# Attention and a gated two-layer product on one core: half sums moved to SBUF, two PSUM pairs, an immediate bias, a third feature buffer and another plan

## The chip, the core and the metric

The kernel runs on one core of one Trainium2 chip. A core has five engines that work side by side, each through its own instruction queue in order: PE (TensorE) multiplies matrices and writes only into PSUM, ACT (ScalarE) evaluates functions and copies, DVE (VectorE) does elementwise work, POOL (GpSimd) here issues DMAs and a few small writes, and SP (SyncE) issues DMAs. PSUM has eight banks of 128 partitions by 512 float32. The metric is the device time of one execution in microseconds, the lower the better.

## The reference, cut to what matters

There are 8 batches with 8 heads of 576 tokens and 64 features each. For each head

```python
q_p, k_p = phi(q, c, s), phi(k, c, s)        # relu(x) * cos(w), relu(x) * sin(w), side by side: 128 features
kv  = einsum('sf,sd->fd', k_p, v)            # 128 x 64
z   = sum(k_p, axis=s)                       # 128
num = q_p @ kv;  den = q_p @ z + 1e-6
attn = num / den
```

The result is laid out as x, 4608 tokens by 512 features, and goes through

```python
h = x @ w_in           # 512 -> 2048
g = h * cos(h)
out = g @ w_out        # 2048 -> 512, float32
```

Inputs and output are float32; on the chip the matmuls take float16 and sum in float32.

## The kernel before, in words

**Tiling.** A batch's 576 tokens are 4 tiles of 128 and a rest of 64. The rests of two batches share a tile, so all rests together form a ninth chunk of 512 tokens. The gated product therefore runs over nine chunks: chunk c is batch c for c below 8, and chunk 8 holds the rests.

**Attention of a batch.** `load` (L354) brings q, k and v by DMA on SP into one raw buffer each, which the next batch uses again. `prep` (L377) makes the features kp and qp, as Relu with a scale on ACT (L386) or as max and multiply on DVE (L387). `cast_v` (L391) casts v. `kv` (L405) sums 8 heads of k features times v and a column of ones (L413) and copies the result to kvz (L425, L427 or L430). The q features are transposed, for the first two batches by PE (`q_pe`, L436), later by DMA (`q_dma`, L450). `num` (L459) computes numerator and denominator in two banks of PSUM (L474) and a DVE norm after it: the denominator (L490), its reciprocal (L492) and the product (L494). The result x is transposed into xT, for batches 0 to 2 by PE (`x_pe`, L507), later by DMA (L522).

**The gated product of a chunk.** `layer1` multiplies by w_in: in column pieces of 256 tokens for chunks 0 and 1 (L561), as whole tiles (L593) for chunk 2, and for the chunks after that half as whole tiles and half by a scheme of seven products of half size instead of eight (`layer1_fast`, L663, matmuls on L695), with intermediate sums on ACT (L703) and DVE (L707). `gate` (L531) takes cos as a sine with a bias of pi/2 that lies in a column of SBUF, PIH, on ACT (L534), and multiplies on DVE (L536) into gT. gT exists twice; chunk c uses gT[c % 2], chunk 8 gT[0]. `layer2` multiplies by w_out, also with seven products (L849), with sums of gT parts on DVE (L831, L876) and results gathered in ost by ACT (L860) and DVE (L864). Only chunk 0 uses `layer2_plain` (L776): for each of four token tiles a first half of eight matmuls (j below 8) and a second half, which sum up in the same bank (L789); the four tiles hold M2_0, M2_1, TR and M1_2 until the second half is done, and then ACT copies each to ost (L796).

**PSUM.** M1_0 to M1_2 and TR serve layer 1 and transposes, M2_0 and M2_1 layer 2, and ATT, two banks wide, the attention. Batch 0's four numerators are spread over pairs of these banks, `PAIRS` (L319), and batch 1's all use ATT.

**Order.** No engine order is written out by hand. Each piece of work is a step of `Plan` (L17), with an engine, an estimated cost, a due time, and the buffers that it reads and writes. `forward` (L92) lays the steps out in time by keys, `backward` (L191) derives new keys from how late each step could be, and `run` (L71) repeats this 12 times and keeps the order with the earliest end. Steps with several engines, such as preps, take the engine that ends first. This happens while the program is built, not on the chip. The first step sequence is `first_attention`, `layer1(0)`, `late_q0`, `second_attention`, `layer2_plain(0)`, `layer1(1)`, `w_out_sums` (L801), and then attention, `layer2` and `layer1` per chunk. w_out arrives in quarters; its second half waits behind batch 1's loads (`rest_of_w_out`, L949).

Of the kernel before, what the change touches and what calls it, by code (L numbers as in the profile page):

```python
# [16 lines left out]
class Plan:  # L17
# [11 lines left out]
    PASSES = 12  # L29
# [11 lines left out]
    def add(self, eng, occ, lat, due, fn, rd=(), wr=(), dma=None, lane=None, late=0.0,  # L41
            lazy=None):
# [17 lines left out]
        for key in wr:  # L60
# [6 lines left out]
                               lazy=lazy))  # L67
# [3 lines left out]
    def run(self):  # L71


        key = [s["due"] for s in self.steps]
        best = None
        for _ in range(self.PASSES):
            start, done = self.forward(key)
            end = max(done)
            if best is None or end < best[0]:
                best = (end, start, done, [s["eng"] for s in self.steps])  # L80
            key = self.backward(start, done, end)
        for s, a, b, e in zip(self.steps, best[1], best[2], best[3]):
            s["start"], s["end"] = a, b
            s.update(zip(("eng", "occ", "lat", "fn"), s["opts"][e]))
        return sorted(self.steps, key=lambda s: (s["start"], s["n"]))
# [6 lines left out]
    def forward(self, key):  # L92
# [13 lines left out]
        ready = {e: [] for e in self.LINK}  # L106

# [20 lines left out]
        while todo:  # L128
            best = None
            for e, cand in ready.items():  # L130
                if not cand:
                    continue
                limit = max(free[e], min(avail[n] for n in cand)) + self.PATIENCE.get(e, 0.0)
                k, t, n = min(((key[n], max(free[e], avail[n]), n) for n in cand
                               if avail[n] <= limit and first(n, e, max(free[e], avail[n]))),
                              default=(0, 0, None))
                if n is None:
                    rest = [(max(free[e], avail[n]), n) for n in cand
                            if first(n, e, max(free[e], avail[n]))]
                    if not rest:  # L140
                        continue
                    t, n = min(rest)
                if best is None or t < best[0]:
                    best = (t, e, n)
# [28 lines left out]
            free[e] = t + s["occ"]  # L173
            if n in follow:
# [59 lines left out]
def kernel(  # L234
# [57 lines left out]
    kp = sb("kp", [P, NT + 1, H, 2, D])  # L292
    qp = sb("qp", [P, NT + 1, H, 2, D])
# [9 lines left out]
    gT = [sb(f"gT{n}", [P, NJT, SM]) for n in range(2)]  # L303
    NCH = 4
# [13 lines left out]
    LEAD = 32.0  # L318
    PAIRS = [(BANKS[0], BANKS[1]), (BANKS2[0], BANKS2[1]), None, (BANKS[2], BANKS[3])]  # L319

# [4 lines left out]
    ORDER0, ORDER1, HOLDW = "qkv", "kqv", 1  # L325
# [12 lines left out]
    def dve(occ, due, fn, rd, wr, lat=0.13, lazy=None):  # L338
        pl.add("DVE", occ, occ + lat, due, fn, rd, wr, lazy=lazy)
# [4 lines left out]
    def either(due, cost, fn, rd, wr):  # L344

        lat = {"DVE": 0.13, "ACT": 0.15, "POOL": 0.15}
        pl.add([(e, cost[e], cost[e] + lat[e], fn[e]) for e in cost], 0, 0, due, None, rd, wr)
# [183 lines left out]
    def gate(bank, key, dst, dkeys, due):  # L531
        c = chn[0] % NCH
        chn[0] += 1
        act(0.59, due, lambda: nc.scalar.activation(  # L534
            out=ch[c], in_=bank, func=AF.Sin, bias=PIH, scale=1.0), [key, "PIH"], [("ch", c)])
        dve(0.61, due, lambda: nc.vector.tensor_tensor(  # L536
            out=dst, in0=bank if len(dst.shape) == 2 else bank.rearrange("p (j s) -> p j s", j=dst.shape[1]),
            in1=ch[c] if len(dst.shape) == 2 else ch[c].rearrange("p (j s) -> p j s", j=dst.shape[1]),
            op=ALU.mult), [key, ("ch", c)], dkeys)
# [47 lines left out]
    def layer1_plain(c, j, X, xk):  # L587
# [8 lines left out]
        gate(M, mk, gT[c % 2][:, j, :], [("g", c % 2, j, t) for t in range(NT)], due + 1.5)  # L596
# [3 lines left out]
    SUMS_AT = min(FAST1) - 1  # L600
    CH2, JF = NCT // 2, JH * P // 2
# [11 lines left out]
    n2 = CH2 * JF  # L613

    def wsum(ap, n):
        return ap[:, n * n2:(n + 1) * n2].rearrange("p (c f) -> p c f", c=CH2)
    WSB = {n: wsum(flat(kp if n in (2, 3) else qp), n % 2) for n in range(1, 5)}
# [9 lines left out]
    def w_in_sums(f, due):  # L627
# [3 lines left out]
        gone = {nm: [(nm + "p", t, g, h) for t in range(NT + 1) for g in range(2) for h in range(H)]  # L631
                for nm in "kq"} if f else {"k": [], "q": []}
        ws = WSB if f else WSA

        def tt(n, a, b, op, rd, wr):
            dve(0.61, due, lambda: nc.vector.tensor_tensor(out=ws[n], in0=a, in1=b, op=op),
                [("w_in", f), ("w_in", 2 + f)] + rd, wr + [("WS", n, f)], lazy=20.0)
        tt(3, a11, a21, ALU.subtract, [], gone["k"])
        tt(1, a21, a22, ALU.add, [], gone["q"] if f else [("w_in", 2)])
        tt(2, ws[1], a11, ALU.subtract, [("WS", 1, f)], [])  # L640
        tt(4, a12, ws[2], ALU.subtract, [("WS", 2, f)], [])

# [3 lines left out]
    def layer1_sums(c, X, xk):  # L646
# [6 lines left out]
        def tt(n, a, b, rd, wr=()):  # L653
            dve(0.33, start[c] - 1 + 0.3 * n, lambda: nc.vector.tensor_tensor(
                out=XS[n], in0=a, in1=b, op=ALU.subtract), xk + rd, [("XS", i, n)] + list(wr))
        tt(0, b12, b11, [], (hk("k") + hk("q") + hk("v") + ["AL"]) if c == B - 1 else ())
# [6 lines left out]
    def layer1_fast(c, g, X, xk):  # L663

        G = gT[c % 2]
# [44 lines left out]
        def out2(due):  # L710
# [7 lines left out]
            act(0.95, due, lambda: nc.scalar.activation(  # L718
                out=cc2, in_=uz, func=AF.Sin, bias=PIH, scale=1.0), [zk[1], zk[2], "PIH"], ck)
            g4 = G.rearrange("p (h j) s -> p h j s", h=2)[:, :, j0:j0 + 2, TH:SM]  # L720

            def four(ap):
                return ap.rearrange("p (h j s) -> p h j s", h=2, j=2)
            dve(1.14, due, lambda: nc.vector.tensor_tensor(
                out=g4, in0=four(uz), in1=four(cc2), op=ALU.mult), [zk[1], zk[2], *ck],
                [("g", c % 2, h * JH + j, t) for h in range(2) for j in (j0, j0 + 1) for t in (2, 3)])

        def out(src_, key, hj, ht, due):
            js = slice(hj * JH + j0, hj * JH + j0 + 2)
            gate(src_, key, G[:, js, ht * TH:(ht + 1) * TH],  # L730
                 [("g", c % 2, j, t) for j in range(js.start, js.stop)
                  for t in (2 * ht, 2 * ht + 1)], due + 1.5)
# [4 lines left out]
        out(Y, zk[0], 0, 0, d)  # L737
# [38 lines left out]
    def layer2_plain(c):  # L776
        G = gT[c % 2]
        w0 = start[c] + width[c]
        bank = BANKS2 + [BANKS[3], BANKS[2]]
        os_ = [on[0] % NO, (on[0] + 1) % NO]  # L780
        on[0] += 2
        for jh in range(2):
            for n, t in enumerate(range(NT) if jh == 0 else (3, 2, 0, 1)):
                due = w0 + (jh * NT + n) * 1.8
                M, mk = bank[t]

                def mm(M=M, t=t, jh=jh):
                    for j in range(jh * JH, (jh + 1) * JH):
                        nc.tensor.matmul(M, lhsT=G[:, j, t * P:(t + 1) * P], rhs=w_out_sb[:, j, :],  # L789
                                         start=(j == 0), stop=(j == NJT - 1))  # L790
# [3 lines left out]
                if jh == 1:  # L794
                    o = os_[t // 2]
                    act(0.5, due + 1.0, lambda O=ost[o], t=t, M=M: nc.scalar.activation(  # L796
                        out=O[:, t % 2, :], in_=M, func=AF.Copy), [mk], [("ost", o, t % 2)])
# [3 lines left out]
    def w_out_sums():  # L801
# [5 lines left out]
        def tt(out_, a, b, op, rd, wr):  # L807
            dve(1.14, start[2] - 8, lambda: nc.vector.tensor_tensor(
                out=out_, in0=a, in1=b, op=op), rd, wr)
# [5 lines left out]
    def layer2(c):  # L815

        G, W = gT[c % 2], w_out_sb
        lo, hi = slice(0, JH), slice(JH, NJT)
        a11, a12 = G[:, lo, 0:TH], G[:, hi, 0:TH]
        a21, a22 = G[:, lo, TH:SM], G[:, hi, TH:SM]  # L820
        w0, ww = (start[c + 1], width[c + 1]) if c < B else (start[c] + width[c], 14.0)

        def gk(hj, ht, js=range(JH)):
            return [("g", c % 2, hj * JH + j, 2 * ht + t) for j in js for t in range(2)]
        NG = 2 if c == B else 1
        for q_ in range(NG):
# [3 lines left out]
            def tt(out_, a, b, op, rd, wr, due, sl=sl):  # L830
                dve(0.07 + 1.07 / NG, due, lambda: nc.vector.tensor_tensor(  # L831
                    out=out_[:, sl], in0=a[:, sl], in1=b[:, sl], op=op), rd, wr)
# [40 lines left out]
        for q_ in range(NG):  # L873
# [4 lines left out]
                gk(1, 0, js) + [("S2", q_)], gk(1, 0, js))  # L878
# [40 lines left out]
    def weights():  # L919
# [14 lines left out]
        pl.add("POOL", 0.2, 0.3, 0, hold2, [("w_in", 1)], [("w_out", g) for g in range(4)])  # L934
        w_out_load(0, 2)
# [13 lines left out]
    def rest_of_w_out(nm):  # L949
        def hold():  # L950
            nc.gpsimd.tensor_copy(
                out=w_out_sb[0:1, JH:, 0].rearrange("p (g j) -> p g j", g=2)[:, :, 0],
                in_=raw[nm][0:1, 0, 0, 0:1].broadcast_to((1, 2)))
        pl.add("POOL", 0.2, 0.3, 0, hold, hk(nm), [("w_out", g) for g in (2, 3)])
        w_out_load(2, 4)
# [25 lines left out]
    def second_attention():  # L981
        T = start[1] - 30
        for nm in ORDER1:
            hold_raw(nm)
            load(1, nm, T, HALVES if nm == ORDER1[2] else (slice(0, H),))
# [102 lines left out]
```

## Time and profile before

| what | value |
|---|---|
| median of 3 runs | 288.9 us (288.8 to 293.18) |
| profiled execution | 286.95 us, of it span 285.2 us |
| granted TensorE clock, mean | 0.992 |
| PE matmuls | 270.4 us busy, 95% of the span, 2604 |
| PE weight loads | 207.9 us, 73% |
| DVE | 247.5 us, 87% |
| ACT | 222.1 us, 78% |
| POOL | 26.1 us, 9% |
| HBM | 36.74 MB read, 9.44 MB written |

The span runs from the first to the last instruction of the program; 1.75 us of the profiled execution's own time lies around it. A row of a group of instructions names the line, the engine, the output and the inputs, their shapes and their number. Matmuls are pipelined, so the duration of one is longer than the time from its start to the next one's; where it matters the text uses times from start to start. The time of idle before an instruction stands in brackets behind it with what ended it.

### The profile page before, as it was taken

The page shows a single profiled execution, that of the slowest core. Times are in us where ns is not written, and L with a number is a line of the kernel's source. Part 1 is how long each engine was busy: PE and PEld are TensorE (multiplying, and loading weights), DVE is VectorE, ACT ScalarE, POOL GpSimd, SP SyncE. Part 2 cuts the span into 40 slices and gives each one's busy share as a digit, 9 for nine tenths or more (in the row PEclk, how much of TensorE's full clock was granted, in tenths as well). Part 3 has the DMA queues.
Part 4 walks back from the last instruction along what each step waited for, and adds up shares of the span by engine and source line. Part 5 has one row for each costly group of instructions (what it writes and reads, how often), then busy time and mean ns, then how long its engine had stood idle before and what let it go on. Part 6 is the DMA issues. An engine that isn't in the chain of part 4 may idle for free.

```text
span 285.2 us, 6555 instructions
## 1 busy us (share of the span) xinstructions
PE 270.4 (95%) x2604; PEld 207.9 (73%) x2604; DVE 247.5 (87%) x454; ACT 222.1 (78%) x361; POOL 26.1 (9%) x53
## 2 busy tenths in 40 slices
PE   6668988999999999999999999999999999999993
PEld 2457956569975679777877787787877876876783
DVE  2876887998999999999999999999799989976941
ACT  2845897999999999899999999999854676467410
POOL 1412020011000011001100200020002000100200
PEclk9997999999999999999999999999999999999999
DMA  6999999799958999996999599939444000300214
GB/s 211 299 201 272 253 307 307 245 304 300 227 168 158 327 149 300 181 327 106 298 187 312 106 358 266 229 85 204 92 39 153 34 18 3 148 2 0 98 52 147
DMA packets 77566, 53.29 MB, mean 187 GB/s; under 512 B 46048, under 2 KB 75232, under 8 KB 77536
## 3 DMA queue, kind: packets, MB, share of 16 engines
q1 hardware_dynamic: 70032, 39.73, 57.2%
q0 software_dynamic: 6784, 12.59, 17.1%
q10 hardware_dynamic: 720, 0.57, 0.6%
q8 instruction: 20, 0.33, 0.5%
q14 instruction: 10, 0.08, 0.1%
HBM read 36.74 MB, written 9.44 MB: 162 GB/s over the span
## 4 chain that ended last, share of the span: by engine, by line
PE 86%; DVE 5%; DMA 3%; ACT 3%; issue 1%; SPq 0%; DVEq 0%; ACTq 0%
PE M L849 34%; PE M L593 16%; PE M L695 9%; PE M L561 9%; PE TR L695 4%; PE TR L593 4%; PE ATT L474 3%; DMA km<-in_k_dram 3%; PE ATT L413 3%; PE M L789 2%; DVE kp L387 2%; PE TR L789 1%; DVE x L494 1%; DVE gT L536 1%; ACT qp L386 1%
## 5 line engine op out<-in xcount | busy, mean ns | idle before, releaser
L534 ACT ACTIVATE ch<-M,PIH 128x512 f32<-128x512 f32 x90 | 60.6, 685 | 13.4 <-PE M L561 6.1
L849 PEld LDWEIGHTS <-gT 128*128 128x128 f16 x640 | 62.1, 98 | 11.3 <-issue 0.3
L536 DVE TENSOR_TENSOR gT<-M,ch 128x512 f16<-128x512 f32 x90 | 60.2, 683 | 5.7 <-ACT ch L534 5.2
L849 PE MATMUL M<-w_out_sb,gT 128*128 128x256 f16 x512 | 63.1, 273 | 0.2 <-ACT ost L860 0.2
L593 PE MATMUL M<-xT,w_in_sb 128*128 128x512 f16 x184 | 45.7, 379 | 0.0
L386 ACT ACTIVATE qp<-qm,CS 128x512 f16<-128x512 f32 x59 | 40.1, 718 | 4.4 <-DMA qm<-in_q_dram 4.4
L593 PEld LDWEIGHTS <-w_in_sb 128*128 128x128 f16 x256 | 24.2, 98 | 19.7
L758 POOL DMA_DIRECT2D out_dram<-ost x32 | 17.2, 541 | 216.0 <-DVE ost L864 108.0
L386 ACT ACTIVATE kp<-km,CS 128x512 f16<-128x512 f32 x51 | 34.6, 718 | 1.2 <-DMA km<-in_k_dram 1.2
L561 PE MATMUL M<-xT,w_in_sb 128*128 128x256 f16 x256 | 31.4, 278 | 1.7 <-DVE gT L536 0.9
L849 PE MATMUL M<-T,S 128*128 128x256 f16 x256 | 32.5, 273 | 0.0
L561 PEld LDWEIGHTS <-w_in_sb 128*128 128x128 f16 x256 | 25.0, 100 | 5.6 <-issue 2.1
L860 ACT ACTIVATE ost<-M 128x512 f32<-128x512 f32 x31 | 18.5, 598 | 12.1 <-PE M L849 12.0
L849 PEld LDWEIGHTS <-S 128*128 128x128 f16 x256 | 24.8, 98 | 3.5
L494 DVE TENSOR_TENSOR x<-ATT,rec 128x512 f16<-128x512 f32 x33 | 22.8, 691 | 1.1
L695 PEld LDWEIGHTS <-w_in_sb 128*128 128x128 f16 x192 | 18.5, 98 | 4.5
L864 DVE TENSOR_TENSOR ost<-M,ost 128x512 f32<-128x512 f32 x24 | 16.4, 681 | 5.2 <-issue 3.8
L831 DVE TENSOR_TENSOR S<-gT 128x2048 f16<-128x2048 f16 (+1 forms) x18 | 19.7, 1100 | 0.2
L474 PEld LDWEIGHTS <-qT 128*128 128x128 f16 x320 | 14.9, 98 | 4.2 <-issue 1.5
L695 PEld LDWEIGHTS <-WS 128*128 128x128 f16 x144 | 13.7, 98 | 3.6
L707 DVE TENSOR_TENSOR Z<-M,Z 128x512 f32<-128x512 f32 x23 | 15.5, 683 | 0.8 <-PE M L695 0.4
L474 PE MATMUL ATT<-kvz,qT 128*128 128x65 f16 x296 | 15.1, 193 | 0.8 <-DVE x L494 0.8
(122 smaller groups left out, 392.0 us busy)
## 6 DMA issues: line engine op xcount, KB each, us to landing
out_dram<-ost POOLq DMA_DIRECT2D x32, 256.0 KB, 4.2
qm<-in_q_dram SPq DMA_DIRECT2D x8, 640.0 KB, 6.1
km<-in_k_dram SPq DMA_DIRECT2D x8, 640.0 KB, 8.1
qm<-in_q_dram SPq DMA_DIRECT2D x8, 512.0 KB, 5.7
km<-in_k_dram SPq DMA_DIRECT2D x8, 512.0 KB, 6.5
vm<-in_v_dram SPq DMA_DIRECT2D x6, 640.0 KB, 6.5
vm<-in_v_dram SPq DMA_DIRECT2D x6, 512.0 KB, 6.7
w_in_sb<-in_moe_w_in_dram POOLq DMA_DIRECT2D x4, 512.0 KB, 8.7
```

Source lines behind the costliest of these rows:

```text
L386: fn = {"ACT": lambda: nc.scalar.activation(out=out_, in_=in_, func=AF.Relu, scale=sc), "DVE": lambda: nc.vector.tensor_scalar(out=out_, i ...
L474: nc.tensor.matmul(bank[hb][:, hh * D1:(hh + 1) * D1], lhsT=a[:, h, :], rhs=z[:, h, :], start=(i == 0), stop=(i == len(parts) - 1))
L494: nc.vector.tensor_tensor(out=split(x16[n][:, hs, :], k), in0=A[:, :, :, 0:D], in1=split(rec[n][:, hs], k).unsqueeze(3).broadcast_to((P, k ...
L534: act(0.59, due, lambda: nc.scalar.activation(out=ch[c], in_=bank, func=AF.Sin, bias=PIH, scale=1.0), [key, "PIH"], [("ch", c)])
L536: dve(0.61, due, lambda: nc.vector.tensor_tensor(out=dst, in0=bank if len(dst.shape) == 2 else bank.rearrange("p (j s) -> p j s", j=dst.sh ...
L561: nc.tensor.matmul(M1[m][:, jj * 2 * P:(jj + 1) * 2 * P], lhsT=w_in_sb[:, cc, j * P:(j + 1) * P], rhs=X[:, cc, ts], start=(cc == 0), stop= ...
L593: nc.tensor.matmul(M, lhsT=w_in_sb[:, cc, j * P:(j + 1) * P], rhs=X[:, cc, :], start=(cc == 0), stop=(cc == NCT - 1))
L695: nc.tensor.matmul(bank[0][:, j * TH:(j + 1) * TH], lhsT=a(cc, j), rhs=b[:, cc, :], start=(first and j == 0 and cc == 0), stop=(last and j ...
L758: pl.add(eng, 0.9 if eng == "POOL" else 0.65, 0, due, lambda: q.dma_start(out=dst, in_=src_), keys, [], dma=(nb, 355.0))
L831: dve(0.07 + 1.07 / NG, due, lambda: nc.vector.tensor_tensor(out=out_[:, sl], in0=a[:, sl], in1=b[:, sl], op=op), rd, wr)
L849: nc.tensor.matmul(bank[0][:, tt * MH:(tt + 1) * MH], lhsT=a[:, j, tt * P:(tt + 1) * P], rhs=b[:, j, :], start=(first and tt == 0 and j == 0),
L860: act(0.5, due, lambda: nc.scalar.activation(out=dst, in_=view(bank), func=AF.Copy), [bank[1]], dk)
```

## The change

The edits are these.

- **Half sums of chunk 0.** `layer2_plain` no longer keeps four banks. Each half of a token tile is a sum of its own in M2_0 or M2_1 by turns. ACT copies the first half's to ost (L841 of the new kernel), DVE adds the second half's (L844).
- **Two PSUM pairs for batch 1.** `second_attention` gives its numerators ATT and the pair M1_2/TR by turns (`PAIRS1`).
- **Immediate bias.** The sine takes pi/2 as a constant of the instruction, in `gate` and in `layer1_fast`; PIH is used only by the first sine of the program. The planner's cost of a sine goes from 0.59 to 0.5 and from 0.95 to 0.86.
- **Chunk 8 in feature buffers.** kp and qp become the halves of one tile, KQ, and chunk 8's gated layer is written there instead of to gT[0] (`G2`, `gi`). The steps that make its sums wait until the features are no longer read.
- **Finer sums.** `layer2` makes its sums in two parts for chunk 7 too (`NG`).
- **Plan.** `run` adds 97 rounds to the 12 passes. Each disturbs the keys within a random stretch of time by a random amount, runs four passes, and goes on from there if the end is at most 0.02 later; the earliest end found is used. The seed is fixed.
- **Without effect as set.** A `port` mark that keeps DVE and POOL from working at once, and a `mul` that could run on POOL, are added, but no step of either kind goes to POOL (`Y_POOL`, `UZ_POOL` empty). `W_FIRST` is None. `WSB`, sums for a second part of w_in that no chunk uses, moves to qT.

```diff
-    PASSES = 12
+    PASSES, ROUNDS = 12, 97
...
+        best = [math.inf]
+        rnd = random.Random(1)
+
+        def passes(key, n):
+            local = None
+            for _ in range(n):
+                start, done = self.forward(key)
+                end = max(done)
+                if end < best[0]:
+                    best[:] = [end, start, done, [s["eng"] for s in self.steps]]
+                key = self.backward(start, done, end)
+                if local is None or end < local[0]:
+                    local = end, key
+            return local
+        now = passes([s["due"] for s in self.steps], self.PASSES)
+        for _ in range(self.ROUNDS):
+            amp, wide = rnd.choice((0.5, 1, 2, 4)), rnd.choice((20, 40, 80, 300))
+            mid = rnd.uniform(0, best[0])
+            key = [k + (rnd.gauss(0, amp) if abs(k - mid) < wide / 2 else 0) for k in now[1]]
+            new = passes(key, 4)
+            if new[0] < now[0] + 0.02:
+                now = new
...
-    kp = sb("kp", [P, NT + 1, H, 2, D])
-    qp = sb("qp", [P, NT + 1, H, 2, D])
+    KQ = sb("KQ", [P, 2, (NT + 1) * H * 2 * D])
+    kp, qp = [KQ[:, n].rearrange("p (t h g d) -> p t h g d", t=NT + 1, h=H, g=2) for n in range(2)]
...
+    G2 = [g.rearrange("p (h j) s -> p h j s", h=2) for g in gT]
+    G2.append(KQ[:, :, 0:JH * SM].rearrange("p h (j s) -> p h j s", j=JH))
...
+    BANKS_L2 = (BANKS2, BANKS2)
     PAIRS = [(BANKS[0], BANKS[1]), (BANKS2[0], BANKS2[1]), None, (BANKS[2], BANKS[3])]
+    PAIRS1 = (None, PAIRS[3])
...
-        act(0.59, due, lambda: nc.scalar.activation(
-            out=ch[c], in_=bank, func=AF.Sin, bias=PIH, scale=1.0), [key, "PIH"], [("ch", c)])
+        act(0.5, due, lambda: nc.scalar.activation(
+            out=ch[c], in_=bank, func=AF.Sin, bias=math.pi / 2.0, scale=1.0), [key], [("ch", c)])
...
+    def gi(c):
+        return c % 2 if c < B else 2
...
     def layer2_plain(c):
+
         G = gT[c % 2]
         w0 = start[c] + width[c]
-        bank = BANKS2 + [BANKS[3], BANKS[2]]
         os_ = [on[0] % NO, (on[0] + 1) % NO]
         on[0] += 2
         for jh in range(2):
-            for n, t in enumerate(range(NT) if jh == 0 else (3, 2, 0, 1)):
+            for n, t in enumerate(range(NT)):
                 due = w0 + (jh * NT + n) * 1.8
-                M, mk = bank[t]
+                M, mk = BANKS_L2[jh][n % len(BANKS_L2[jh])]
 
                 def mm(M=M, t=t, jh=jh):
                     for j in range(jh * JH, (jh + 1) * JH):
                         nc.tensor.matmul(M, lhsT=G[:, j, t * P:(t + 1) * P], rhs=w_out_sb[:, j, :],
-                                         start=(j == 0), stop=(j == NJT - 1))
+                                         start=(j == jh * JH), stop=(j == (jh + 1) * JH - 1))
...
-                if jh == 1:
-                    o = os_[t // 2]
-                    act(0.5, due + 1.0, lambda O=ost[o], t=t, M=M: nc.scalar.activation(
-                        out=O[:, t % 2, :], in_=M, func=AF.Copy), [mk], [("ost", o, t % 2)])
+                o = os_[t // 2]
+                O, ok = ost[o][:, t % 2, :], ("ost", o, t % 2)
+                if jh == 0:
+                    act(0.5, due + 1.0, lambda O=O, M=M: nc.scalar.activation(
+                        out=O, in_=M, func=AF.Copy), [mk], [ok])
+                else:
+                    dve(0.61, due + 1.0, lambda O=O, M=M: nc.vector.tensor_tensor(
+                        out=O, in0=M, in1=O, op=ALU.add), [mk, ok], [ok])
...
-        NG = 2 if c == B else 1
+        NG = 2 if c >= B - 1 else 1
...
-            n = num(1, t, due)
+            n = num(1, t, due, PAIRS1[t % len(PAIRS1)])
```

**What the built programs show of the order.** PE has the same 2604 matmuls of the same forms. Up to batch 1's numerators its order is nearly the old one. Then numerators 1 and 0 stand side by side in M1_2/TR and ATT, the third group of `layer2_plain`'s first halves follows on M2_0, and the fourth on M2_1, before chunk 1's layer 1 begins; the second halves come between its first pieces. On DVE the gate that released M1_0 for the last piece of chunk 0's layer 1 stands ahead of two k preps of batch 1 instead of behind three. On ACT there are 114 preps instead of 110 and 21 v casts instead of 19. On SP the q transposes of batch 2 stand ahead of batch 3's loads of v and q; on POOL the order of the loads is the same, and the stores follow ost0, ost1, ost2 by turns.

## The prediction

> **What bounds the kernel now.** I read the busy time by stage first, because the shares over the whole span mix stages. The columns are the stretch, its length, busy us of each engine, granted TensorE clock, DMA share and GB/s.
>
> ```profile
> 14.00:25.00 11.00, 8.14 (x104) 6.00 (x105) 8.23 (x28) 5.56 (x11) 2.48 (x7) 0.84 1.19 210
> 25.00:38.00 13.00, 11.96 (x112) 10.61 (x112) 10.45 (x18) 10.39 (x17) 2.85 (x6) 1.00 1.14 290
> 38.00:48.00 10.00, 8.81 (x120) 6.49 (x120) 7.71 (x21) 9.60 (x17) 0.00 (x0) 1.00 1.16 277
> 48.00:60.00 12.00, 11.87 (x103) 7.21 (x103) 11.04 (x22) 9.32 (x18) 0.96 (x2) 1.00 0.84 279
> 60.00:82.00 22.00, 22.00 (x274) 19.19 (x273) 20.54 (x43) 20.89 (x37) 1.39 (x3) 1.00 1.00 262
> 82.00:200.00 118.00, 117.80 (x1158) 90.35 (x1155) 114.05 (x204) 113.86 (x186) 8.46 (x16) 1.00 0.96 222
> 200.00:281.00 81.00, 80.72 (x688) 63.65 (x685) 67.83 (x107) 44.92 (x71) 6.35 (x12) 1.00 0.21 58
> ```
>
> From 48 us on, PE is idle 0.6 us in 233. Busy alone could hide slow matmuls, so I then took two pieces of the chain that ended last:
>
> ```profile
> 82.57 2.59 PE M L593 x12
> 266.75 13.99 PE M L849 x128
> ```
>
> 2.59/12 = 0.216 and 13.99/128 = 0.109 us from start to start. The Trainium skill (Perfetto Trace Analysis, Identifying the Most-Contended Engine) warns against matmul busy time and wants LDWEIGHTS busy share instead: that is 73% here, and would leave 27% of 285.2, 77 us, to win. The start-to-start times decide against it: 0.216 for 512 columns is exactly twice 0.109 for 256, and the usual times from start to start of each form, times their counts, add up to 262.7 us. Only 22.5 us of the span is anything else: 1.3 before the first matmul, 4.6 after the last, and 16.6 lost between starts. Of that about 10 lie in the first 20 us, behind the load of batch 0, and 2.5 between 20 and 25. Later ones worth naming are 1.05 at 37 us and, in the timeline of PE (start, duration, instruction, idle time before it), two near 47:
>
> ```profile
> 45.82 0.42 PE L474 MATMUL ATT<-kvz,qT 128*128 128x65 f16 x8
> 46.08 0.61 PE L442 MATMUL M<-IDENT,qp 128*128 128x128 f16 x8
> 47.53 0.42 PE L474 MATMUL ATT<-kvz,qT 128*128 128x65 f16 x8 [0.84 <-DVE x L494]
> 48.13 1.89 PE L789 MATMUL M<-w_out_sb,gT 128*128 128x512 f16 x8 [0.18 <-DVE gT L536]
> ```
>
> Eight transposes issue in 0.45 us (0.61 counts the drain), so PE lost 47.53-46.53 = 1.0 us until the norm emptied ATT, and 48.13-47.79 = 0.34 until bank M1_2 was released. What pins this stretch is seen on ACT and DVE:
>
> ```profile
> 42.68 0.70 DVE L401 CAST V<-vm 128x256 f16<-128x256 f32 x3 [0.18 <-DMA vm<-in_v_dram]
> 42.95 0.71 ACT L400 ACTIVATE V<-vm 128x256 f16<-128x256 f32 x2
> 43.56 0.71 ACT L386 ACTIVATE qp<-qm,CS 128x512 f16<-128x512 f32 x1
> 44.25 1.02 ACT L446 ACTIVATE qT<-M 128x1024 f16<-128x1024 f16 x1
> 45.17 0.60 ACT L430 ACTIVATE kvz<-ATT 128x520 f16<-128x520 f32 x1
> ```
>
> Batch 1's last v lands at 42.59; four ACT steps later kvz is written (45.77), and only then can batch 1's numerators start.
>
> **The change, part by part.** PE executes the same matmuls, so 262.7 stays. What can move is gaps.
>
> *Two PSUM pairs and half sums together.* In the new order ACT still does, after v lands, two casts, one prep, the qT copy and kvz: 42.65 + 0.7 + 0.65 + 1.02 + 0.6 (with overlaps) = 45.7. So the pin stays. After it the old PE order, up to 56.44, holds 10.62 us: four numerators (0.26 each from start to start), one q transpose (0.45), four x transposes (0.22), four L789 groups (1.72): 9.3 of work, 1.33 idle. Two of the L789 groups (second half) and one x transpose come later in the new order; without them the old one would reach this point at 56.44-3.45-0.22 = 52.77. The new order from the pin: numerator 1 in M1_2/TR and numerator 0 in ATT at once, to 46.3. Then the third first-half group on M2_0, whose copy to ost stands right behind kvz on ACT (0.6, 46.3), so no wait: to 48.1. Numerator 3 needs norm 1 (DVE 46.2 to 47.5: two dens, rec, two half-size multiplies), met. Numerator 2 needs norm 0 in ATT (1.05 later, 48.55), met within 0.15. Two x transposes, the fourth group (to 50.8), one more: 51.1. The last q transpose has gone into the wait for v. Gain: 52.77-51.1 = 1.65. It doesn't rest on what PE does before: were PE late by the whole 1.05, it would still meet the pin within 0.3.
>
> *The gap at 37 us* (gate behind three k preps on DVE). In the new order that gate stands ahead of the preps, worth 1.05 by itself, but PE then waits longer for v: about 1.3 of idle between 41 and 45.7. I count it at nothing. Here the skill (TensorE: Matmul & The Clock Gate, on the idle and busy windows) speaks against the change: an idle window of about 3.4 us halves the clock, and 3.4 us at half rate is up to 1.7 us of lost work, all of the gain. The trace shows the effect once: after the idle start the clock in 14 to 25 is 0.84, and eight 256-column matmuls take 1.72 instead of 0.87. But 38 to 48 with 1.2 us idle is at 1.00, and the new idle is as much in pieces. I take the row, zero, and keep 1.7 for the range.
>
> *What half sums add.* Four ACT copies take the place of four (0.59 each): nothing. Four DVE adds (0.61 from issue to issue: 2.44) are new, and two paired norms (0.28 each): 3.0. One 1024-wide v cast (0.6) leaves DVE in this stretch. DVE idle from 48 to 82 is 0.96+1.46 = 2.4, so it is about full. Add 0 waits for PE; queued behind it are add 1, a w_out sum (1.15), a v cast and the first gate of chunk 1's layer 1, which holds bank M1_2. Replayed with these durations, add 0 ends at 56.6 and PE needs its bank at 57.3; add 1 at 57.2 against 59.9; that gate at 59.6 against 61.6. So hidden, by 0.7 at the tightest. With the second half 1.6 earlier throughout, PE reaches chunk 2's layer 1 (82.40 before) at about 80.8.
>
> *Immediate bias.* A sine from PSUM takes 685 ns, a copy of the same size without a per-partition operand 598; a Relu with a scale operand 718, a copy of that size 630. The 88 ns fits the operand, not the function. 120 sines of 512 and 12 of 1024: 11.6 us of ACT. Four preps and two casts more on ACT take 4 back. ACT ends no wait that PE feels after 48, except 0.2 at 106.6: worth 0 to 0.4, I take 0.
>
> *Last layer in feature buffers, finer sums.* From 200 to 281 PE is idle 0.28 us: nothing to gain; each split DVE sum costs 0.07 (four, 0.3), covered by DVE's 13 us idle there. Below nothing only if a sum comes late in the last 14 us; DVE is nearly idle then. 0.
>
> *The shaken plan* does no work on the chip but orders everything. SP issues as many DMAs, but batch 2's q transposes now go ahead of batch 3's v and q. Before, they were behind the v loads and the first landed at 68.5, when PE took it at 69.67. The new order wants it at 67.2. Ahead of two loads that landed at 66.1 and 67.5 it should be there; if not, 1.3 is lost. POOL's order is the same except that stores of chunk 0 follow adds.
>
> Sum: profiled execution 286.95 (span 285.2 and 1.75 around it) - 1.65 = 285.3; on the median 288.9, which lies 1.95 above the profiled one: **287.3**.
>
> **Rivals.** *Handed back* (0.22): after 48 the plan has no gaps to spare, and xT lands only some 2 us before its use in several chunks (134.67 and 136.95; 162.06 and 164.11; 190.38 and 192.81), paced by DMA. Then PE waits there instead: 1.3 to 1.6 lost, 288.7. For: DMA share 0.96 from 82 to 200. Against: SP's order was moved too.
> *The opening and small gaps go as well* (0.16): of the 2.5 us between 20 and 25 one or two, plus 0.4 at 106; 285.5. For: the fourth x transpose is moved ahead of a layer 1 group. Against: v's landing pins what follows.
> *Slower* (0.12): add 0 in the DVE queue. It stands behind four k preps that wait for batch 2's k (landed 50.12), two w_out sums and a norm. If it ends later than 57.3, PE stands; from 2.3 us later on (k after about 52.5) the whole gain is gone and each further us costs one. With 4 late: 290.6.
> *The bias doesn't shorten a sine* (0.04): ACT, idle 6.1 us between 50 and 200, must take 4.1 more; 289.
>
> **How the numbers follow.** The likeliest case, 287.3, has 0.46; alone it spans 286.4 to 288.2. With the other cases the range is 285.2 to 289.8, where the 1.7 of a cold clock is held too. Faster by over 2% (below 283.1, about what a measurement here can tell from no change) needs 5.8 us, nearly every gap after 14 us: 0.04. Slower by over 2% (above 294.7) needs several waits at once: 0.03.
>
> **What would show it.** Right: no wait of the numerators for the norm, chunk 2's layer 1 starting near 80.8, sines at about 600 ns, the last long L896 run starting 1.6 earlier. Wrong: PE waits for an add at L844, for qT near 67, or for xT; clock below 1.00 after 40; v of batch 1 landing elsewhere than 42.6.

## The result, and the profile after

The kernel after takes 285.91 us in the median (285.15 to 286.6, 4 runs), the kernel before 288.85 (288.8 to 293.62, 4 runs) on the same chip; the ratio is 0.9898 [0.9854, 0.9941], where the brackets hold the 95% interval. Two more measurements gave 285.49 against 287.61, ratio 0.9911 [0.9876, 0.9946], and 285.76 against 287.38, ratio 0.9944 [0.9913, 0.9975]. So the change saves 0.6 to 1.0%, and 1.6 to 2.1 us of the median in the two larger measurements. The forecast was 287.3, range 285.2 to 289.8, within 2%. Here and below, medians and ratios leave out executions more than 1.5% above the kernel's fastest (in these three measurements 2 of 4, 16 of 54 and 24 of 68 of the kernel before, none of the kernel after), while ranges and numbers of runs are of all.

The profiled executions differ by less: 285.83 us with a span of 284.0, against 286.95 and 285.2. First the busy time by stage of the kernel after, in the columns of before (stretch, length, PE, weight loads, DVE, ACT, POOL, granted clock, DMA share, GB/s):

```profile
14.00:25.00 11.00, 7.67 (x102) 5.89 (x103) 6.46 (x25) 4.15 (x9) 2.67 (x7) 0.78 1.21 216
25.00:38.00 13.00, 12.75 (x111) 10.82 (x110) 9.95 (x17) 9.62 (x17) 2.55 (x5) 0.92 1.14 298
38.00:48.00 10.00, 9.72 (x131) 7.23 (x129) 8.79 (x24) 9.91 (x19) 0.00 (x0) 1.00 1.16 287
48.00:60.00 12.00, 12.00 (x108) 7.41 (x107) 11.62 (x27) 9.44 (x18) 1.55 (x2) 1.00 0.58 189
60.00:82.00 22.00, 22.00 (x248) 18.53 (x246) 21.04 (x42) 21.05 (x37) 1.06 (x2) 1.00 1.08 295
82.00:200.00 118.00, 118.00 (x1192) 91.83 (x1191) 113.53 (x200) 111.32 (x192) 8.47 (x16) 1.00 1.01 227
```

From 48 to 200 us PE is never idle. From 38 to 48 its idle time went from 1.19 to 0.28. But the granted clock fell from 0.84 to 0.78 in the first row, and to 0.92 in the second, where it had been 1.00. In the chain that ended last (start, length, engine, tile, line, count):

```profile
80.58 2.66 PE M L635 x12
83.24 1.21 PE ATT L445 x40
...
265.63 13.99 PE M L896 x128
```

Chunk 2's layer 1 begins at 80.58 (82.57 before), and the last long run 1.1 earlier than before. The first of these is only in part a gain: the 40 matmuls of k features times v (1.21 us) now stand behind that layer's first group; in the chain of before they stood ahead of it:

```profile
81.36 1.21 PE ATT L413 x40
```

The place that the prediction replayed, on ACT and then on PE:

```profile
45.79 0.60 ACT L462 ACTIVATE kvz<-ATT 128x520 f16<-128x520 f32 x1
```

```profile
46.76 0.29 PE L506 MATMUL TR<-kvz,qT 128*128 128x65 f16 x4
46.89 0.29 PE L506 MATMUL M<-kvz,qT 128*128 128x65 f16 x4
47.02 0.42 PE L506 MATMUL ATT<-kvz,qT 128*128 128x65 f16 x8
47.28 1.89 PE L833 MATMUL M<-w_out_sb,gT 128*128 128x512 f16 x8
```

Numerators 1 and 0 run side by side and no bracket stands behind the output group: both waits of before, 0.84 for the norm and 0.18 for the gate, are gone. The sines, before and after:

```profile
L534 ACT ACTIVATE ch<-M,PIH 128x512 f32<-128x512 f32 x90 | 60.6, 685 | 13.4 <-PE M L561 6.1
L576 ACT ACTIVATE ch<-M 128x512 f32<-128x512 f32 x90 | 52.8, 595 | 14.8 <-PE M L635 7.0
```

595 ns in place of 685, and ACT is 214.9 us busy in place of 222.1.

**Where the time went, in one table.** As in the prediction, every matmul's distance to the next start is compared with the usual one of its form. The usual ones sum to 262.3 to 262.7 us in every profile without added matmuls; apart from 1.3 us before the first start and 4.7 behind the last, the rest is PE's lost time, here by stretches of the span (us), beside the half clock that the trace shows in the first 30 us.

| profile | span | half clock at | 0–30 | 30–40 | 40–60 | 60–end | lost |
|---|---|---|---|---|---|---|---|
| before | 285.2 | 21.4–24.8 | 12.37 | 1.07 | 1.76 | 1.36 | 16.55 |
| after | 284.0 | 20.2–27.0 | 13.29 | 0.49 | 0.68 | 1.02 | 15.49 |
| after, third measurement | 282.4 | 21.1–24.5 | 11.90 | 0.19 | 0.64 | 1.03 | 13.78 |
| before, immediate bias alone | 283.6 | none | 11.38 | 0.55 | 1.78 | 1.36 | 15.05 |
| before, shaken plan alone | 283.4 | none | 11.33 | 0.10 | 2.14 | 1.19 | 14.77 |
| after, plan not shaken | 283.3 | none | 11.00 | 1.62 | 0.53 | 1.56 | 14.72 |

The two rows with one 3.4 us stretch of half clock each, before and the third measurement, are alike in clock (0.992 and 0.991). They differ by 2.8 us: 0.5 in the first 30, 0.9 in 30 to 40, 1.1 in 40 to 60, 0.3 behind it. The kernel after's first profile has two such stretches, and its first 30 us lose 1.4 more.

### The profile page after: what moved, and what is told of

It reads as the page before. It is cut to its first block, busy times and chain, and to the rows that moved or that the text cites. A ratio compares the mean times of both kernels' runs of the same rounds, so it can differ in the third digit from the quotient of the medians.

```text
span 284.0 us, 6561 instructions
## 1 busy us (share of the span) xinstructions
PE 271.6 (96%) x2604; PEld 208.8 (74%) x2604; DVE 248.1 (87%) x460; ACT 214.9 (76%) x367; POOL 26.8 (9%) x53
## 4 chain that ended last, share of the span: by engine, by line
PE 89%; DVE 6%; DMA 2%; ACT 1%; issue 1%; DVEq 0%
PE M L896 34%; PE M L635 16%; PE M L739 9%; PE M L603 9%; PE M L833 5%; PE TR L739 4%; PE TR L635 4%; PE ATT L506 3%; PE ATT L445 3%; DVE KQ L419 2%; DMA qm<-in_q_dram 2%; DVE V L433 1%; PE M L546 1%; DVE gT L578 1%; DVE qT L480 1%
## 5 line engine op out<-in xcount | busy, mean ns | idle before, releaser
L576 ACT ACTIVATE ch<-M 128x512 f32<-128x512 f32 x90 | 52.8, 595 | 14.8 <-PE M L635 7.0
L578 DVE TENSOR_TENSOR gT<-M,ch 128x512 f16<-128x512 f32 x83 | 55.1, 684 | 7.1 <-ACT ch L576 6.8
L896 PEld LDWEIGHTS <-gT 128*128 128x128 f16 x560 | 54.0, 98 | 9.9
L896 PE MATMUL M<-w_out_sb,gT 128*128 128x256 f16 x448 | 55.8, 273 | 0.0
L418 ACT ACTIVATE KQ<-qm,CS 128x512 f16<-128x512 f32 x58 | 39.1, 719 | 4.1 <-DMA qm<-in_q_dram 4.1
L418 ACT ACTIVATE KQ<-km,CS 128x512 f16<-128x512 f32 x56 | 38.0, 717 | 0.0
L603 PE MATMUL M<-xT,w_in_sb 128*128 128x256 f16 x256 | 32.7, 285 | 0.9 <-ACT xT L550 0.7
L526 DVE TENSOR_TENSOR x<-ATT,rec 128x512 f16<-128x512 f32 x31 | 21.4, 691 | 1.1
L506 PEld LDWEIGHTS <-qT 128*128 128x128 f16 x320 | 15.6, 98 | 4.8 <-issue 1.2
L878 DVE TENSOR_TENSOR S<-gT 128x2048 f16<-128x2048 f16 (+1 forms) x16 | 17.3, 1086 | 0.1
```

The source lines that it names most:

```text
L418: fn = {"ACT": lambda: nc.scalar.activation(out=out_, in_=in_, func=AF.Relu, scale=sc), "DVE": lambda: nc.vector.tensor_scalar(out=out_, i ...
L506: nc.tensor.matmul(bank[hb][:, hh * D1:(hh + 1) * D1], lhsT=a[:, h, :], rhs=z[:, h, :], start=(i == 0), stop=(i == len(parts) - 1))
L526: nc.vector.tensor_tensor(out=split(x16[n][:, hs, :], k), in0=A[:, :, :, 0:D], in1=split(rec[n][:, hs], k).unsqueeze(3).broadcast_to((P, k ...
L576: act(0.5, due, lambda: nc.scalar.activation(out=ch[c], in_=bank, func=AF.Sin, bias=math.pi / 2.0, scale=1.0), [key], [("ch", c)])
L578: mul(due, 0.61, lambda q: q.tensor_tensor(out=dst, in0=bank if len(dst.shape) == 2 else bank.rearrange("p (j s) -> p j s", j=dst.shape[1] ...
L603: nc.tensor.matmul(M1[m][:, jj * 2 * P:(jj + 1) * 2 * P], lhsT=w_in_sb[:, cc, j * P:(j + 1) * P], rhs=X[:, cc, ts], start=(cc == 0), stop= ...
```

## The experiments

**The kernel after again**, with no edit, first beside the three that follow, later a third time.

> The changed kernel once more, beside the kernel before on the same chip, to separate two readings of the first comparison. Theory A (the gain is the stretch from 40 to 52 us and the gap at 106): the median lies 1.0 to 1.8 us below that of before in pairs of executions with a like clock, and the rest of the first difference is the clock of single executions. Theory B (the gain is 3 us or more and real): the medians differ by 2.8 us or more in every round.

> The kernel after once more, beside the next three on the same chip. Theory A: median 285.5, as in the second measurement, all executions between 284 and 287, while those of the kernel before reach from 285 to 294.

Measured: 285.49 (284.13 to 286.65, 9 runs) and 285.76 (284.04 to 288.0, 22 runs); the kernel before beside them 287.61 (285.5 to 293.71, 54 runs) and 287.38 (285.23 to 293.29, 68 runs). Best against best the gain is 1.2 to 1.4, between medians 1.6 to 2.1: nearer to theory A than to B. Part of the kernel before's spread is the granted clock, but not all. Sorted by each execution's mean clock (the kernel before in three measurements, after in two):

| mean granted clock | before: executions, median | after: executions, median |
|---|---|---|
| over 0.995 | 19, 286.0 | none |
| 0.990 to 0.995 | 66, 287.3 | 8, 284.3 |
| 0.983 to 0.989 | 25, 287.5 | 6, 285.9 |
| under 0.983 | 17, 288.9 | 17, 285.8 |

At a like clock the change is worth 1.6 to 3.1 us, on few executions of the kernel after, which never kept its full clock.

**The bias.** In the kernel after's exact order the sine takes its bias from the column again; in the kernel before's exact order it takes the immediate (the diff is the first one; the second is its reverse).

```diff
-            out=ch[c], in_=bank, func=AF.Sin, bias=math.pi / 2.0, scale=1.0), [key], [("ch", c)])
+            out=ch[c], in_=bank, func=AF.Sin, bias=PIH, scale=1.0), [key], [("ch", c)])
...
-                out=cc2, in_=uz, func=AF.Sin, bias=math.pi / 2.0, scale=1.0), [zk[1], zk[2]], ck)
+                out=cc2, in_=uz, func=AF.Sin, bias=PIH, scale=1.0), [zk[1], zk[2]], ck)
```

> The changed kernel in exactly its order, but the sine takes its bias from the SBUF column again. If ACT's time is hidden behind PE, as I hold, the span grows by at most 0.5 us although the sines take 685 instead of 595 ns and ACT is busy some 11 us longer. If the immediate bias carries the gain, the span grows by 1.2 us or more.

> The kernel before in its exact order, with the immediate cosine bias alone. Theory A (ACT ends no wait that PE feels): sines of 595 ns in place of 685, ACT about 11.6 us less busy, span 0 to 0.4 less in executions with a like clock, the spread as in the kernel before (some 3 in 10 above 290 us); median 288 to 289. Rival F (a slow ACT is what makes the long executions of the kernel before): they are gone, median near 287.

```profile
L576 ACT ACTIVATE ch<-M,PIH 128x512 f32<-128x512 f32 x90 | 60.6, 694 | 11.3 <-PE M L635 5.5
```

With the column a sine takes 694 ns again and the kernel 286.12 (284.99 to 287.94, 20 runs), 0.4 to 0.6 over the kernel after (0.2 to 1.2 by drawing the executions again at random); PE's lost time behind 30 us is 2.8, where three profiles of the kernel after have 1.9 to 2.4. With the immediate alone in the old order: sines of 595 ns and 287.65 (22 runs) against 287.52 in the same measurement, ratio 1.0027 [0.9992, 1.0061], and 6 of 22 executions still above 290. So 90 ns less on each sine gave nothing in the old order, and some 0.5 in the new. The second expectation's rival, that a slow ACT makes the long executions, falls.

**Plan and edits apart.** The kernel before with the new `run`, and the kernel after with `ROUNDS` at 0.

```diff
-    PASSES, ROUNDS = 12, 97
+    PASSES, ROUNDS = 12, 0
```

> The kernel before with nothing but the 97 disturbed rounds of the plan, costs and buffers as before. If the plan alone brings the gain, the span falls by 1.0 us or more. If the second PSUM pair and the free banks are what it takes, the waits near 47 us stay and the span falls by less than 0.6 us.

> The changed kernel with the 12 passes only, no disturbed rounds. If the structural edits alone bring the gain, the span stays within 0.5 us of the changed kernel's. If the plan is what it takes, the span returns to that of before or lies above it.

286.54 (284.87 to 290.04, 20 runs), ratio 0.9952 [0.9921, 0.9984], and 286.59 (285.05 to 288.59, 12 runs), ratio 0.9972 [0.994, 1.0005]. Beside the 287.61 of the kernel before in the same measurement each alone gains 1.0 to 1.1, and both together 2.1: in the medians they simply add up. PE's timeline shows what each lacks; without the edits:

```profile
43.99 0.42 PE L491 MATMUL ATT<-kvz,qT 128*128 128x65 f16 x8 [0.69 <-ACT kvz L447]
...
50.71 0.42 PE L491 MATMUL ATT<-kvz,qT 128*128 128x65 f16 x8 [1.00 <-DVE x L511]
```

and without the shaking:

```profile
37.39 1.90 PE L833 MATMUL M<-w_out_sb,gT 128*128 128x512 f16 x8 [1.38 <-DMA w_out_sb<-in_moe_w_out_dram]
```

The shaken plan alone clears 37 us (0.10 lost in 30 to 40) and still waits for the norm in ATT. The edits alone clear that (0.53 in 40 to 60), but their plan takes an output group before its w_out has landed. Each alone loses 2.2 us in 30 to 60, both together 0.8 to 1.2, the kernel before 2.8; in single profiles of this stretch both together save more than the sum.

**The second pair.** The kernel after in its exact order, batch 1's numerators all in ATT. They then overwrite each other for part of batch 1's rows, which are not the reference's; the amount of work is the same.

```diff
-        bank = [p[0] for p in pair] if pair else [ATT[:, hb, :] for hb in range(2)]
+        bank = [p[0] for p in pair] if pair and b != 1 else [ATT[:, hb, :] for hb in range(2)]
```

> The kernel after in its exact order, but batch 1's numerators all go into ATT again, as before. Theory A (the second PSUM pair is what took the 1.0 us wait for the norm away): PE waits 0.8 to 1.1 us for DVE's norm between 46.5 and 48.5, the new order offers nothing that fills it, and the span grows by 0.8 to 1.2; median near 286.5. Rival B (the order alone took it away, by putting an output group between the numerators): a wait under 0.3, the span within 0.3.

```profile
47.05 0.29 PE L506 MATMUL ATT<-kvz,qT 128*128 128x65 f16 x4 [1.42 <-DVE x L526]
...
50.68 0.29 PE L506 MATMUL ATT<-kvz,qT 128*128 128x65 f16 x4 [1.12 <-DVE x L526]
```

Two waits, 2.5 us, where one of 0.8 to 1.1 was expected: the new order issues two tiles' numerators right behind each other, twice. The median is 288.55 (18 runs), the lost time in 40 to 60 is 3.41 in place of 0.64 to 0.68. The rival, that order alone took the wait away, falls. The half sums were not tested apart from the plan. The old order's single wait is not what the pair is worth here: the new order is built on it.

**Where batch 3's v stands on SP.** In the kernel after's order its two loads go ahead of batch 2's q transposes again. In the kernel before's order they go behind them, and two of batch 3's v casts move to the last one, so that DVE doesn't wait for the later loads. `LOADS` and `QDMA` hold the numbers of the plan's steps.

```diff
-        for s in pl.run():
+        plan = pl.run()
+        early = [s for s in plan if s["n"] in LOADS[3, "v"]]
+        plan = [s for s in plan if s["n"] not in LOADS[3, "v"]]
+        at = [s["n"] for s in plan].index(QDMA[2, 0])
...
+        for s in plan[:at] + early + plan[at:]:
             s["fn"]()
```

and for the second

```diff
-        for s in pl.run():
+        plan = pl.run()
...
+        for s in plan:
+            if s["n"] == last:
+                order += [part[n] for n in sorted(set(CASTS[3]) - {last}, key=where.index)]
+            if s["n"] not in moved:
+                order.append(s)
+            if s["n"] == QDMA[2, 3]:
+                order += [part[n] for n in sorted(LOADS[3, "v"], key=where.index)]
...
+        for s in order:
             s["fn"]()
```

> The kernel after, with one thing put back on SP's queue: batch 3's two v loads are issued ahead of batch 2's four q transposes, where the kernel before has them; the order on the other engines stays. In the kernel after these transposes land 1.8 to 4.0 us ahead of their numerators, in the one before only 1.0 to 1.2 ahead. Theory D (the executions of the kernel before that take 290 us and more are those in which PE waits for a late q transpose): the first transpose lands near 68.5 and PE waits 0.5 to 1.5 us for it at 68 to 72; median 287 to 288, and some executions above 289. Theory E (the long executions come from elsewhere): a wait of at most 0.5 us near 68, median near 286, no execution above 288.

> The kernel before with three moves and nothing else: on SP batch 3's two v loads are issued behind batch 2's four q transposes, and on DVE two of batch 3's three v casts stand later, next to the last one near 78 us, so that they don't wait for the later load. Theory D (the late q transposes make the long executions): the transposes land some 2 us earlier and no numerator of batch 2 waits; executions above 290 go from some 3 in 10 to less than 1 in 10, median near 287. Rival G (another transfer makes them, as much as this one): the median within 0.5 of the kernel before, with the same long executions.

In the first:

```profile
69.99 0.43 PE L509 MATMUL ATT<-kvz,qT 128*128 128x65 f16 x8 [1.45 <-DMA qT<-KQ]
```

PE waits 1.45 us for the transpose, and the median is 288.2 (286.15 to 290.38, 22 runs). That is 2.7 and 2.4 over the kernel after in its two larger measurements (it did not run beside this one), and 7 of 22 executions lie above 289 where those have none. Theory D holds for this order: the place of two loads on SP decides over some 2.4 us. Its executions don't spread wider (4.2 us, against 4.0 in the third measurement); they are later as a whole. In the second, the numerators of batch 2 run without a wait (they start at 68.11, 70.34, 72.57 and 75.67), a wait of 0.35 for DVE is new at 84, and the median is 287.54 (14 runs) against 287.38, ratio 1.0011 [0.9973, 1.0049]: no gain. Above 290 is 1 of 14, where the kernel before has 17 of 68. With 14 executions this could be chance. So it is not shown that these transposes make the kernel before's long executions.

**Add 0 late.** Two sums of 1.2 us, read by nobody, ahead of the first new add in DVE's queue.

```diff
+            if s["n"] == ADDS[0]:
+                for _ in range(2):
+                    nc.vector.tensor_tensor(out=S3, in0=w_out_sb[:, 0:JH, 0:MH],
+                                            in1=w_out_sb[:, JH:, 0:MH], op=ALU.add)
             s["fn"]()
```

> The kernel after with two sums of 2048 elements a partition (1.15 us each on DVE, into a buffer that is not yet in use, read by nobody) put into DVE's queue right ahead of add 0, the first of the four new adds. By the prediction's replay add 0 has 0.7 us to spare until PE needs its bank; the trace of the kernel after shows some 0.8. Theory H (that slack is all there is): PE waits 1.4 to 1.7 us for the bank near 58 and the span grows by 1.4 to 1.7. Rival: DVE's later work has no slack left and the delay grows on its way through the gates of chunk 1 (2.3 and more), or something gives way and less than 1 us is seen.

DVE and then PE:

```profile
50.59 1.67 DVE L419 TENSOR_SCALAR KQ<-km,CS 128x512 f16<-128x512 f32 x4 [0.69 <-DMA km<-in_k_dram]
...
55.68 2.47 DVE L1112 TENSOR_TENSOR S<-w_out_sb 128x2048 f16<-128x2048 f16 x2
58.07 1.28 DVE L846 TENSOR_TENSOR ost<-M,ost 128x512 f32<-128x512 f32 x2
```

```profile
58.81 1.89 PE L834 MATMUL M<-w_out_sb,gT 128*128 128x512 f16 x8 [2.34 <-DVE ost L846]
```

2.34 us of wait from 2.4 of added work: in this execution nothing was spare. The first row says why: the chain runs from batch 2's k, which landed at 50.49 here, through four preps, two sums and a norm into add 0. In the third measurement k landed at 49.33, and there add 0 ended at 55.75 with its bank wanted at 56.48. Here, without the sums, it would have ended at 55.68 + 0.68 = 56.36, and PE was ready for the bank at 56.30. So the margin is 0.7 or nothing, by when k lands. In the median the edit costs 1.7 (287.5, 20 runs, against 285.76), as theory H has it. From the gate of chunk 1 on, nothing grew.

**The opening.** Zero matmuls, which nobody reads, where PE waits in the opening: 16 behind batch 0's x transposes, and in a second kernel 18 more, 8 and 10 behind the two groups of zero matmuls that were there.

```diff
+        KEEP = {XPE[0, 0]: (M1[1], 6), XPE[0, 2]: (ATT[:, 0, :], 5), XPE[0, 1]: (ATT[:, 0, :], 5)}
         for s in pl.run():
             s["fn"]()
+            if s["n"] in KEEP:
+                bank, n = KEEP[s["n"]]
+                for _ in range(n):
+                    nc.tensor.matmul(bank[:, 0:TH], lhsT=WZ[:, 0:P], rhs=WZ[:, 0:TH],
+                                     start=True, stop=True)
```

> The kernel after with 16 matmuls of zeros, 256 columns each, whose results nobody reads: 6 behind the first x transpose of batch 0, 5 each behind the next two, where PE waits for a norm or a copy anyway. Theory C (in the opening the new order leaves PE idle so long that its clock drops to half from 20.2 to 27.0 us, where the order without shaking lost none; this took back a part of the gain): the granted clock is 1.00 from 14 to 27 us, layer 1 of chunk 0 takes 0.109 us from start to start from its first group on, and the span is 1.0 to 1.5 less than the 283.9 of the kernel after; median near 284.3. Rival: the clock drops as before or the added matmuls stand in the way; the span within 0.4 of 283.9, or longer.

> The kernel after with the 16 matmuls of zeros of the previous opening experiment and 18 more of 256 columns: 8 behind the first group of zero matmuls that both kernels start with, 10 behind the second, where PE waits for a prep and for a cast of v. Theory C (what the new order costs in the opening is the half clock): no stretch of half clock that falls on work that counts from 6 us on, batch 0's attention not delayed, median 283.5, that is 1.5 to 2.5 below the kernel after on the same chip, and less spread. Rival: the 18 added ones stand in the way or the half clock moves elsewhere; 284.6 as with 16, or more.

With 16, the clock is 1.00 from 14 us on, but in this execution a half-clock stretch lies at 8.3 to 11.7, where batch 0's 24 q transposes take 2.7 us in place of 1.5 and its v casts come later, so that the k times v matmuls begin at 15.48 where they began at 14.43. The median is 284.61 (283.54 to 285.5, 17 runs), ratio to before 0.9911 [0.9886, 0.9936]; the kernel after was not run beside it. With 34 there is no half clock from 7.3 us to 280:

```profile
14.00:25.00 11.00, 9.14 (x131) 7.45 (x132) 7.57 (x28) 5.01 (x12) 2.77 (x7) 1.00 1.21 215
25.00:38.00 13.00, 13.00 (x118) 10.98 (x116) 10.82 (x19) 11.37 (x20) 2.31 (x5) 1.00 1.14 295
```

Chunk 0's layer 1 is done, and the first output group begins, at 36.73 (after: 39.43 and 37.78; before: 39.10, and 37.57 in a profile without half clock). The median is 284.91 (283.74 to 288.85, 22 runs), 0.8 below the kernel after's beside it; the ratios to before, 0.9909 [0.9879, 0.9939] and 0.9944 [0.9913, 0.9975], overlap, so the gain in the median is not settled. Theory C holds in its mechanism, that the full clock brings layer 1 forward, not in the 1.5 to 2.5 it named. What came instead is in the same profile:

```profile
169.48 0.43 PE L506 MATMUL ATT<-kvz,qT 128*128 128x65 f16 x8 [1.03 <-DMA qT<-KQ]
```

PE waits 1.03 us for a late q transpose. The five executions with a mean clock of 1.000 alone take 284.2 to 287.9. The clock can't do that; a late transfer is what this one profile shows of it.

## Why the prediction was right, and where not

**The bound, and the class.** PE's sum of 262.7 held, and what moved were gaps, as said. The change of less than 2% is right; 287.3 was 1.4 too high.

**Two pairs and half sums: 1.65.** The replay was right from the first numerator on: no wait for the norm, none for the bank. From there to chunk 1's layer 1 it is 5.23 us in three profiles of the kernel after, and 6.95 in three of the old order, less the 3.67 that the replay took off: 1.72. But the numerators began later than it said: kvz was written at 46.4 where it had 45.7, and the third output group began at 47.28 where it had 46.3. "The last q transpose has gone into the wait for v" is the term that failed. That wait did not come, so its 0.45 stayed as work ahead of the numerators, and PE lost 0.45 there, for a q copy of DVE, where the old order lost 0.27. So the size was 1.1: 1.76, 1.78 and 1.72 lost from 40 to 60 in the three profiles with the old order, 0.64 to 0.68 in the new. Chunk 2's layer 1 close to the 80.8 named was luck: 1.2 of the 2.0 us by which it came earlier is the 40 matmuls that went behind it.

**The gap at 37: "I count it at nothing".** This step failed. It rested on v's landing at 42.59 as a pin that what comes earlier can't move. Already in the kernel before the pin had 0.36 of slack: ACT took the last v casts at 42.95 without standing idle, at the end of a queue that had run since a sine at 39.30, and that sine had waited for PE. In the kernel after no engine stands idle for v. The chain goes through PE's own work:

```profile
39.59 3.45 PE M L833 x16
43.05 0.46 PE M L474 x8
...
43.56 0.57 issue
44.14 0.69 DVE V L433 x3
...
45.22 0.61 DVE qT L480
...
45.87 1.05 PE M L474 x16
```

and the q copy on DVE, ahead of the last v casts in its queue, waits for PE's transposes:

```profile
43.53 0.69 DVE L480 COPY qT<-M 128x1024 f16<-128x1024 f16 x1 [0.39 <-PE M L474]
```

DVE takes these casts at 44.14, 2.0 us after v landed at 42.16 (1.7 after it in the third measurement). So what opens earlier stays earlier: from the first output group to the numerators it is 7.3 us in both profiles, although one gets there 1.6 earlier, and PE lost 0.45 on the way, not 1.3. The landing moves as well: 42.16, 41.81 and 40.78 in three profiles of the kernel after, 41.17 and 41.05 in two of the old order. The stretch 30 to 40 went from 1.07 (0.55, 0.71) to 0.49 and 0.19. What moves v's landing was not tried.

**The opening** was not a part of the sum at all, only of a rival. At a like clock it gained 0.5. But the new order leaves PE idler between 17 and 21 us, so it runs longer at half clock: 6.8 us in the first profile, whose first 30 us lost 0.9 more than before. The prediction kept the cost of a cold clock in the range and looked for it at 38 to 48, where the clock stayed at 1.00; it came at 20 to 27. The 0.84 of before, which it put down to the idle start, was such a stretch too, at 21.4 to 24.8.

**The step to the median.** "on the median 288.9, which lies 1.95 above the profiled one" was the largest error. That 288.9 was the middle of three executions. In the larger measurements the kernel before's median is 287.4 to 287.6, 0.4 to 0.7 above the profiled one, and the kernel after's 285.83 lies within 0.4 of its own. Carried over, the distance put 1.95 on a kernel that doesn't have it. The errors of the other terms partly cancelled, which is luck: the profiled execution, 285.3 in the sum, came at 285.83, with the gap at 37 better than said and the opening and the pair worse.

**Bias: 0 to 0.4.** Right as an ACT saving that PE doesn't feel: nothing in the old order. About 0.5 in the new. The 0.37 at 105 us that I thought it might win stayed with the bias alone, and went with the new order.

**Last layer, finer sums: 0.** Behind 200 us PE loses 0.20 (0.17 before). No run took them apart.

**Shaken plan.** Batch 2's first q transpose landed at 66.2 and was wanted at 68.0, so it was there. That this place on SP mattered was right, and so was the size in a profile: 1.45 of wait where 1.3 was named. In the median it was 2.4.

**The rivals.** "The opening and small gaps go as well" (285.5) is nearest to what came, at a like clock by 0.9 at the gap at 37, 0.5 in the opening and 0.3 at 105. "Handed back" at xT did not come: behind 60 us 1.02 is lost in place of 1.36. "Slower" through add 0: the chain and its place were right, and so was the margin of 0.7, in some executions; k landed at 49.3 to 50.5, never near 52.5. "The bias doesn't shorten a sine" falls.

What stays open: which wait makes the kernel before take 290 us and more at a clock at which others of its executions take 287. No profile fell on such an execution. Behind the moved v loads a late transpose does this to the new order; that it does so to the old one is argued, not shown.

## What to carry to other kernels

When an edit and a new order come together, run each alone and look at the waits that each leaves: here the order cleared one place, the edit another. When a prediction goes from a profiled execution to a median, first ask on how many executions the median rests and where the profiled one lies among them. A landing time is a pin only where an engine stands idle for it: look at what else held the instruction that took the data.

## What the hardware showed that was not expected

The half clock came in steps of 3.4 us, as the Trainium skill (TensorE: Matmul & The Clock Gate, What's actually happening) has it, but not after an idle window of that length. In the 3.4 us before each drop near 20 us PE was never idle for more than 0.9 us at a time. Worked out from the starts and the usual times of the forms, it was busy for 0.23 to 0.29 of that window in seven profiles of the new order, and each of them dropped. In five profiles of the other orders (before, its immediate bias, its moved loads, the unshaken plan, its shaken plan) the least busy window between 14 and 25 us had 0.37 to 0.42; of these the first dropped (0.37) and four did not. With the added matmuls it was 0.52 and 0.58, and neither dropped there. So here the share of busy time went with the drop, and the old opening stood near the edge.
